# Keys turned on TensorE instead of VectorE, weight words split without GpSimd, and more of them split during the first attention

## The chip, the cores and the metric

The kernel runs on one core of one Trainium2 chip. The metric is the device time of one execution in microseconds. An execution uses five engines with an instruction queue each, all served in order: TensorE (PE, with its weight loads PEld), VectorE (DVE), ScalarE (ACT), GpSimd (POOL) and SyncE (SP), which here only issues DMAs. ScalarE issues some DMAs too. Sixteen DMA engines carry out the transfers of all queues.

## The reference

```python
def sm_attn(qq, kk, vv):
    s = scale * np.matmul(qq, kk.transpose(0, 1, 3, 2))
    s = s - np.max(s, axis=-1, keepdims=True)
    a = np.exp(s)
    a = a / (np.sum(a, axis=-1, keepdims=True) + 1e-09)
    return np.matmul(a, vv)

p_packed = sm_attn(p, k, v)             # 32 packed queries read 576 keys; batch 8, heads 8, width 64
out = sm_attn(q, p_packed, p_packed)    # 576 queries read the 32 packed values
x = out.transpose(0, 2, 1, 3).reshape(4608, 512)
h = x @ w_in;  x = (h * np.cos(h)) @ w_out          # first layer, 512 -> 2048 -> 512
h = x @ w_in2                                       # second layer, the same sizes
P = a[0] + a[1] * h + a[2] * h**2 + a[3] * h**3
Q = 1.0 + abs(b[0]) * abs(h) + abs(b[1]) * h**2
return (P / (Q + 1e-6)) @ w_out2
```

The four weight matrices are given in 64-bit floating point; everything else is fp32.

## The kernel before

**Precision.** The large products use TensorE's fp32r type. An operand is kept as two tiles, a rounded `hi` and a rest `lo`, and each product is three matmuls (hi·hi, hi·lo, lo·hi; `PASSES`). `split` (line 65) makes the pair from fp32 data: a copy on ScalarE and a difference on VectorE. `convert` (line 74) makes it from 64-bit weights, 128x512 of them at a time. It sees each weight as two 32-bit words, `up` and `dn`, interleaved in memory. ScalarE turns `dn` into a scaled float (line 80); VectorE makes an fp32 number of `up` by shifts and masks (lines 82 and 87) and takes its exponent out (line 90); GpSimd multiplies the scaled `dn` by that power of two (line 91); VectorE adds it (line 92); ScalarE rounds the sum to `hi` (line 93); GpSimd takes the difference `lo` (line 94). There are 64 such conversions: 16 of the first layer's input weights (`conv_w1i`), 16 of its output weights (`conv_w1o`) and 32 of the second layer's (`conv_w2`). The words come by a 512 KB load each (`load_st`, tag `st64`, three buffers); for the first layer ScalarE's queue issues it.

**Stage one, the attention (lines 125 to 450).** The 64 heads go in 16 groups of four. For a group `n`, `load_k` and `load_v` fetch its keys and values (SP's queue; two buffers for k, three for v). `prep` turns k with two VectorE transposes of 32x32 blocks (line 185). The packed queries `p` are loaded once (line 149), and VectorE sets them into a block-diagonal tile `pbd` (lines 169 to 176). `s1` makes the scores of four heads in four fp32 matmuls of 288 columns with all 128 rows (line 194), takes the maximum on VectorE (line 208) and the exponential on ScalarE (line 213). The score tile is two PSUM banks with two buffers. `et` turns the exponentials on TensorE by six transposes (line 229); `pv` multiplies them with v in four column tiles (line 242); `ppt` turns the packed values and splits them into `wl` (lines 264 to 279). PSUM's eight banks are all taken: four by `s1`, two by `et`, one each by `pv` and `pt`. Inside the same loop run the conversions: `cvs` lists them in order, `conv_next` does the next and starts the load three places on. There are `NA` = `OF` + `RING` = 7 + 3 = 10 that belong to this stage, at two of three steps of the loop. The second attention of batch 0 (`attn2_steps`, line 307) runs in its last steps and borrows the score tile's PSUM.

**Stage two, the folding (lines 645 to 660).** `wunit(x)` multiplies the packed values of all batches with one 128x512 piece of the first layer's input weights, 12 matmuls and four copies, and stores the four results to DRAM (`wd`); `load_wq` reads them back, and they take the place of attention times weights. 16 units, with the remaining conversions between them: a piece for `RING` units ahead, an output-weight conversion at nine of the units (`more`), and the first four slots of the next stage.

**Stage three, the first layer (128 slots, line 613).** Each slot has 12 matmuls of `h` (line 537), a chain over ScalarE and VectorE for h·cos h (lines 556 to 572), and 24 matmuls of `y` (line 584) of two slots before. The second attention of the next batch and, at every third slot, one of the 32 conversions of the second layer's weights run beside it. **Stage four, the second layer (144 slots, lines 680 to 778)** has neither attention nor conversions.

The order on each engine is set ahead of the run by a planner that simulates the instructions (line 804). It keeps dependencies and may move an instruction past others of the program; `hold` (line 54) ties some to an earlier matmul in that order.

Of the kernel before, what the change touches and what calls it, by code (L numbers as in the profile page):

```python
# [20 lines left out]
def pack_attention_moe_moe_kernel(  # L21
# [14 lines left out]
    nc = tc.nc  # L36
    B, H, S, D = q.shape
    M = p.shape[2]
# [35 lines left out]
    def convert(hi, lo, wd64, pool, n, until=None):  # L74
        up, dn = wd64[:, :, 1], wd64[:, :, 0]
        f = pool.tile([128, n], U32, tag="cvf", bufs=2, name="cvf")
        pw = pool.tile([128, n], U32, tag="cvp", bufs=2, name="cvp")
        dl = dn.bitcast(F32)
        ff, pf = f.bitcast(F32), pw.bitcast(F32)
        hold(nc.scalar.activation(out=dl, in_=dn, func=AF.Copy, scale=2.0 ** -52), until)  # L80
        hold(
            nc.vector.tensor_scalar(  # L82
                out=f, in0=up, scalar1=3, scalar2=0x3FFFFFFF, op0=ALU.logical_shift_left, op1=ALU.bitwise_and
            ),
            until,
        )
        nc.vector.scalar_tensor_tensor(  # L87
            out=f, in0=up, scalar=0xC0000000, in1=f, op0=ALU.bitwise_and, op1=ALU.bitwise_or
        )
        nc.vector.tensor_scalar(out=pw, in0=f, scalar1=0xFF800000, scalar2=None, op0=ALU.bitwise_and)  # L90
        nc.gpsimd.tensor_tensor(out=pf, in0=dl, in1=pf, op=ALU.mult)  # L91
        nc.vector.tensor_tensor(out=ff, in0=ff, in1=pf, op=ALU.add)
        nc.scalar.activation(out=hi, in_=ff, func=AF.Copy)
        nc.gpsimd.tensor_tensor(out=lo, in0=ff, in1=hi.bitcast(F32), op=ALU.subtract)
# [18 lines left out]
    if True:  # L113
# [35 lines left out]
        nc.sync.dma_start(out=px, in_=p.rearrange("b (g h) m d -> (h m) (b g) d", g=G))  # L149
        nc.sync.dma_start(out=par[:, 0:4], in_=pa.unsqueeze(0).to_broadcast([128, 4]))  # L150
        nc.sync.dma_start(out=par[:, 4:6], in_=pb.unsqueeze(0).to_broadcast([128, 2]))
        nc.vector.tensor_scalar(out=coef[:, 0:4], in0=par[:, 0:4], scalar1=-1.0, scalar2=None, op0=ALU.mult)
# [9 lines left out]
        make_identity(nc, ident)  # L162
# [5 lines left out]

        pbd = wv.tile([128, NG, NDB, 4, M], F32, name="pbd")
        nc.gpsimd.memset(pbd, 0.0)  # L170
        for n0, n1 in ((0, 2), (2, NG)):
            for h in range(4):
                nc.vector.transpose(
                    out=pbd[32 * h:32 * h + 32, n0:n1, :, h],
                    in_=px[32 * h:32 * h + 32, n0:n1].rearrange("p n (e i) -> p n e i", e=NDB),
                )

        kT_t = {}

        def prep(n):  # L180
            b, g = divmod(n, G)
            kT = wk.tile([128, NDB, 6, 3, 32], F32, tag="kT", bufs=2, name="kT")
            kx = kx_t.pop(n)
            for e in range(NDB):
                nc.vector.transpose(  # L185
                    out=kT[:, e].rearrange("p r a j -> p a r j"),
                    in_=kx[:, :, 32 * e:32 * e + 32].rearrange("p (a r) i -> p a r i", a=3),
                )
            kT_t[n] = kT.rearrange("p e r a j -> p e (r a j)")
# [11 lines left out]

        E_t, rd_t = {}, {}

        def s1(n):
            ps = ps0.tile([128, 2, 512], F32, tag="s1", bufs=2, name="s1")
            scores(ps, pbd[:, n].rearrange("p e h m -> p e (h m)"), kT_t.pop(n))
# [12 lines left out]
            nc.vector.reciprocal(out=rd, in_=sm)  # L219
            E_t[n], rd_t[n] = E, rd  # L220
# [15 lines left out]
        def pv(n):  # L236
# [3 lines left out]
            for r in range(6):  # L240
                for h in range(4):
# [3 lines left out]
                        rhs=vx[:, h, r * D:r * D + D],  # L245
# [132 lines left out]
        RING = 3  # L378
# [21 lines left out]
        OF = 7  # L400
        cvs = [(load_w1o, conv_w1o, f) for f in range(OF)] + [(load_w1i, conv_w1i, x) for x in range(RING)]
        NA = len(cvs)
        more = (0, 2, 4, 7, 9, 10, 13, 14, 15)
# [16 lines left out]
        for i in range(3):  # L420
# [4 lines left out]
            0, wk, lambda nm: ps0.tile([128, 2, 512], F32, tag="s1", bufs=2, name=nm), tg0, lambda: None  # L425
# [3 lines left out]
        for n in range(NG + 1):  # L429
# [13 lines left out]
            if n % 3 and at_cv[0] < NA:  # L443
                conv_next()
# [156 lines left out]
        a_p.append(wk)  # L601
# [58 lines left out]
        e0.close()  # L660
        at_p = e1t.enter_context(tc.tile_pool(name="at", bufs=1, side="right", **RW))
# [147 lines left out]
```

## Time and profile before

| | |
|---|---|
| median of 3 runs | 1685.23 us (1684.16 to 1691.55) |
| profiled execution | 1685.26 us, span 1683.5 us |
| TensorE busy | 1587.0 us (94% of the span) |
| VectorE busy | 1327.3 us (79%) |
| ScalarE busy | 1197.9 us (71%) |
| GpSimd busy | 184.7 us (11%) |
| granted TensorE clock, mean | 0.979 |

Busy times are those of one profiled execution. Matmuls are pipelined, so the records overlap, and the time of a block of matmuls says more than a record's length. A fp32 matmul shows as two records. In a row of grouped instructions the columns are: line, engine, operation, written tile <- read tiles, shapes, how many; busy time and mean length in ns of one; then the idle time of the engine just before them and what ended it.

### The profile page before, as it was taken

Reading aid. Unit: us, or ns where it says so; the run is one execution under the profiler, and the core shown is the slowest. Engines: PE = TensorE matmul, PEld = TensorE weight load, DVE = VectorE, ACT = ScalarE, POOL = GpSimd, SP = SyncE. Lnnn points to the kernel's source line nnn. Section 1 sums busy time; section 2 is a strip of 40 time slices with the busy share of each in tenths; the row PEclk is TensorE's granted clock in tenths of the full one; section 3 lists DMA queues with packets and bytes.
Section 4 is the critical chain, followed back from the end, with each engine's and each line's share of the span. In section 5 each row is a group of like instructions: output and inputs, shape, how many; then the busy total and the mean of one; then the engine's idle time right before and its main releaser. Section 6 shows DMA issues by size and latency. Waiting matters only on the chain.

```text
span 1683.5 us, 25095 instructions
## 1 busy us (share of the span) xinstructions
PE 1587.0 (94%) x9408; PEld 1382.6 (82%) x9408; DVE 1327.3 (79%) x2054; ACT 1197.9 (71%) x1933; POOL 184.7 (11%) x140
## 2 busy tenths in 40 slices
PE   5677879999999999999999999999999999999996
PEld 3555769999999999999998888888888888888884
DVE  7866977787878787878558888888888888888884
ACT  3345656686767676868668777777787878787874
POOL 4304530121111111221000000000000000000000
PEclk9888899999999999999999999999999999999998
DMA  9977744453435444435183101010100102020100
GB/s 280 260 205 263 254 167 122 129 152 127 141 126 154 140 139 146 137 125 188 62 297 134 52 25 50 26 50 26 51 26 26 50 1 76 1 75 1 45 6 25
DMA packets 104377, 183.57 MB, mean 109 GB/s; under 512 B 12096, under 2 KB 46912, under 8 KB 104256
## 3 DMA queue, kind: packets, MB, share of 16 engines
q1 hardware_dynamic: 97344, 163.09, 30.4%
q10 hardware_dynamic: 6912, 18.88, 3.6%
q8 instruction: 74, 1.21, 0.3%
q14 instruction: 47, 0.39, 0.1%
HBM read 117.97 MB, written 63.96 MB: 108 GB/s over the span
## 4 chain that ended last, share of the span: by engine, by line
PE 81%; DVE 8%; DMA 4%; ACT 3%; issue 2%; POOL 1%; ACTq 0%; SPq 0%; POOLq 0%; DVEq 0%
PE h L689 24%; PE o L747 23%; PE y L584 21%; PE h L537 10%; PE s L194 2%; DMA st<-in_moe_w_in_dram 1%; DVE cvf L87 1%; PE w L290 1%; DVE cvf L82 1%; DMA qx<-in_q_dram 1%; DMA wd<-wev 1%; DVE g L569 1%; DMA px<-in_p_dram 1%; DVE kT L185 1%; ACT u L562 0%
## 5 line engine op out<-in xcount | busy, mean ns | idle before, releaser
L584 PE MATMUL y<-gh,w1o 128*128 128x288 f32 x2048 | 433.3, 298 | 0.8 <-ACT gh L66 0.4
L689 PE MATMUL h<-x,w 128*128 128x512 f32 x1728 | 422.2, 393 | 0.0
L689 PEld LDWEIGHTS h<-x,w 128*128 128x128 f32 x1728 | 324.2, 188 | 74.2
L584 PEld LDWEIGHTS y<-gh,w1o 128*128 128x128 f32 x2048 | 337.2, 189 | 3.4 <-DVE yl L67 1.1
L747 PE MATMUL o<-w,g2h 128*128 128x512 f32 x1152 | 332.9, 393 | 1.2 <-ACT g2h L707 1.2
L584 PE MATMUL y<-gl,w1o 128*128 128x288 f32 x1024 | 297.1, 296 | 2.4 <-DVE gl L67 2.4
L747 PEld LDWEIGHTS o<-w,g2h 128*128 128x128 f32 x1152 | 216.1, 188 | 51.1 <-ACT g2h L707 2.1
L537 PE MATMUL h<-ah,wq 128*128 128x288 f32 x1024 | 227.8, 299 | 15.4 <-DVE g L569 7.1
L747 PE MATMUL o<-w,g2l 128*128 128x512 f32 x576 | 199.9, 393 | 0.0
L722 ACT ACTIVATE sq<-h 128x512 f32<-128x512 f32 x144 | 87.2, 606 | 156.4 <-PE h L689 156.4
L584 PEld LDWEIGHTS y<-gl,w1o 128*128 128x128 f32 x1024 | 193.9, 189 | 3.9 <-DVE gl L67 3.3
L537 PEld LDWEIGHTS h<-ah,wq 128*128 128x128 f32 x1024 | 172.6, 190 | 21.0 <-issue 10.6
L724 DVE SCALAR_TENSOR_TENSOR ab<-sq,coef,ab 128x512 f32<-128x512 f32 x144 | 108.2, 751 | 66.8 <-ACT ab L723 66.6
L562 ACT ACTIVATE u<-h,coef 128x576 f32<-128x576 f32 x128 | 94.2, 737 | 87.7 <-PE h L537 86.9
L537 PE MATMUL h<-al,wq 128*128 128x288 f32 x512 | 151.8, 297 | 0.0
L569 DVE SCALAR_TENSOR_TENSOR g<-h,r 128x576 f32<-128x576 f32 x128 | 96.2, 754 | 61.2 <-ACT r L568 61.0
L91 POOL TENSOR_TENSOR cvp<-st,cvp 128x512 f32<-128x512 f32 x64 | 90.1, 1408 | 442.4 <-DVE cvp L90 191.8
L733 DVE SCALAR_TENSOR_TENSOR ab<-ab,y 128x512 f32<-128x512 f32 x144 | 99.6, 691 | 48.5 <-ACT y L730 48.5
L747 PEld LDWEIGHTS o<-w,g2l 128*128 128x128 f32 x576 | 108.1, 188 | 24.7
L563 DVE SCALAR_TENSOR_TENSOR r<-u,h 128x576 f32<-128x576 f32 x128 | 95.5, 748 | 37.3 <-ACT u L562 36.6
L725 ACT ACTIVATE c<-h,coef 128x512 f32<-128x512 f32 x144 | 113.9, 791 | 8.4 <-DVE g2l L713 8.4
L67 DVE TENSOR_TENSOR gl<-g,gh 128x576 fp32r<-128x576 f32 x128 | 102.8, 803 | 21.4 <-ACT gh L66 19.7
(88 smaller groups left out, 2453.1 us busy)
## 6 DMA issues: line engine op xcount, KB each, us to landing
x<-yd SPq DMA_DIRECT2D x36, 512.0 KB
w<-w2d SPq DMA_DIRECT2D x68, 256.0 KB
wd<-wev SPq DMA_DIRECT2D x64, 256.0 KB
wq<-wd SPq DMA_DIRECT2D x64, 256.0 KB
kx<-in_k_dram SPq DMA_DIRECT2D x16, 576.0 KB
vx<-in_v_dram SPq DMA_DIRECT2D x48, 192.0 KB
qx<-in_q_dram SPq DMA_DIRECT2D x16, 576.0 KB
yd<-yh SPq DMA_DIRECT2D x64, 144.0 KB
```

The costliest lines, as they stand in the source:

```text
L67: lo_eng.tensor_tensor(out=lo, in0=src, in1=hi.bitcast(F32), op=ALU.subtract)
L91: nc.gpsimd.tensor_tensor(out=pf, in0=dl, in1=pf, op=ALU.mult)
L537: last_h[0] = nc.tensor.matmul(out=ps[:, u, 0:HS], lhsT=wq[:, g, a, o:o + 128], rhs=a_t[b, g][c][:, hf * HS:hf * HS + HS], start=(i == 0), ...
L562: nc.scalar.activation(out=u, in_=ph, func=AF.Identity, bias=coef[:, 6:7])
L563: nc.vector.scalar_tensor_tensor(out=r, in0=u, scalar=RND, in1=ph, op0=ALU.subtract, op1=ALU.subtract)
L569: nc.vector.scalar_tensor_tensor(out=gt, in0=ph, scalar=2.0 * math.pi, in1=r, op0=ALU.mult, op1=ALU.mult)
L584: nc.tensor.matmul(out=y_t[d][:, 0:HS], lhsT=w1o_s[f // 4][a][:, f % 4, 128 * d:128 * d + 128], rhs=gs[c][:, u], start=(f == 0 and i == 0) ...
L689: nc.tensor.matmul(out=ps, lhsT=w2_s[f][:, 0, a, 128 * kk:128 * kk + 128], rhs=x_t[t, c, kk], start=(i == 0), stop=(i == 3 * NKD - 1),)
L724: nc.vector.scalar_tensor_tensor(out=ab, in0=sq, scalar=coef[:, 5:6], in1=ab, op0=ALU.mult, op1=ALU.add)
L725: nc.scalar.activation(out=c1, in_=ph, func=AF.Identity, scale=coef[:, 3:4], bias=coef[:, 2:3])
L733: nc.vector.scalar_tensor_tensor(out=ab, in0=ab, scalar=QC, in1=y0, op0=ALU.add, op1=ALU.mult)
L747: nc.tensor.matmul(out=o_t[s], lhsT=g2_t[n][a][:, 128 * s:128 * s + 128], rhs=w2_s[f][:, 1, c], start=(f == 0 and i == 0), stop=(f == NFC ...
```

## The change

1. `convert`: without GpSimd and with one ScalarE instruction in place of two. VectorE's first two instructions make an fp32 number with the low twelve bits of its word cut off (`0x3FFFF000`), so that it is `hi` already; ScalarE copies it. The cut bits (`up & 0x1FF`, in place) and `dn` are put together as integers and scaled by the exponent to `lo`. VectorE has six instructions in place of four.
2. k and p are turned by ten TensorE transposes per group into PSUM (tag `tp`, two buffers of one bank), and ScalarE copies them out in four instructions. The scores are eight matmuls of 64 rows and 32 columns of weights, each in its own tile of the array. The score tile has one buffer in place of two. v's row blocks are read in the order that this makes.
3. p is loaded in two pieces, and doubled along the free axis by VectorE (two groups) and GpSimd (the rest); `pbd` is gone. The identity matrix is made before the first coefficients.
4. `OF` 7 to 12, `RING` 3 to 5: 17 conversions in the attention stage, one at every step of its loop; four output-weight conversions left for the folding stage, at units 11 to 14.
5. The second pair of buffers of the turned attention is allocated after the folding stage instead of before it.

```diff
@@ convert
-        hold(nc.scalar.activation(out=dl, in_=dn, func=AF.Copy, scale=2.0 ** -52), until)
...
-                out=f, in0=up, scalar1=3, scalar2=0x3FFFFFFF, op0=ALU.logical_shift_left, op1=ALU.bitwise_and
+                out=f, in0=up, scalar1=3, scalar2=0x3FFFF000, op0=ALU.logical_shift_left, op1=ALU.bitwise_and
...
+        nc.scalar.activation(out=hi, in_=ff, func=AF.Copy)
+        nc.vector.tensor_scalar(out=up, in0=up, scalar1=0x1FF, scalar2=None, op0=ALU.bitwise_and)
         nc.vector.tensor_scalar(out=pw, in0=f, scalar1=0xFF800000, scalar2=None, op0=ALU.bitwise_and)
-        nc.gpsimd.tensor_tensor(out=pf, in0=dl, in1=pf, op=ALU.mult)
-        nc.vector.tensor_tensor(out=ff, in0=ff, in1=pf, op=ALU.add)
-        nc.scalar.activation(out=hi, in_=ff, func=AF.Copy)
-        nc.gpsimd.tensor_tensor(out=lo, in0=ff, in1=hi.bitcast(F32), op=ALU.subtract)
+        nc.vector.scalar_tensor_tensor(out=q, in0=up, scalar=2.0 ** 32, in1=dn, op0=ALU.mult, op1=ALU.add)
+        nc.vector.scalar_tensor_tensor(out=lo, in0=q, scalar=2.0 ** -52, in1=pf, op0=ALU.mult, op1=ALU.mult)
@@ p
-        nc.sync.dma_start(out=px, in_=p.rearrange("b (g h) m d -> (h m) (b g) d", g=G))
+        pv4 = p.rearrange("b (g h) m d -> (h m) (b g) d", g=G)
+        nc.sync.dma_start(out=px[:, 0:2], in_=pv4[:, 0:2])
+        nc.sync.dma_start(out=px[:, 2:NG], in_=pv4[:, 2:NG])
+        pxx = wv.tile([128, NG, 2, D], F32, name="pxx")
+        for n0, n1, eng in ((0, 2, nc.vector), (2, NG, nc.gpsimd)):
+            eng.tensor_copy(out=pxx[:, n0:n1], in_=px[:, n0:n1].unsqueeze(2).to_broadcast([128, n1 - n0, 2, D]))
@@ prep
-            for e in range(NDB):
-                nc.vector.transpose(
...
+            blocks = [kx[:, a, s].rearrange("p t d -> p (t d)") for s in range(3) for a in range(3)]
+            blocks.append(pxx[:, n].rearrange("p t d -> p (t d)"))
+            for i0 in (0, 4, 8):
+                ps = ps0.tile([128, 4, 128], F32, tag="tp", bufs=2, name="tp")
+                m = min(4, 10 - i0)
+                for i in range(m):
+                    nc.tensor.transpose(ps[:, i], blocks[i0 + i], ident)
+                w = min(4, 9 - i0)
+                nc.scalar.activation(out=kT[:, i0:i0 + w], in_=ps[:, 0:w], func=AF.Copy)
+                if w < m:
+                    nc.scalar.activation(out=pT, in_=ps[:, w], func=AF.Copy)
@@ scores of s1
+        def scores1(ps, kT, pT):
+            for t in range(2):
+                for h in range(4):
+                    nc.tensor.matmul(
+                        out=ps[32 * h:32 * h + 32, t, 0:HS],
+                        lhsT=pT[64 * t:64 * t + 64, 32 * h:32 * h + 32],
+                        rhs=kT[64 * t:64 * t + 64, :, 32 * h:32 * h + 32],
+                        start=True,
+                        stop=True,
+                        tile_position=(64 * t, 32 * h),
+                    )
-            ps = ps0.tile([128, 2, 512], F32, tag="s1", bufs=2, name="s1")
+            ps = ps0.tile([128, 2, 512], F32, tag="s1", bufs=1, name="s1")
@@ plan
-        RING = 3
+        RING = 5
-        OF = 7
+        OF = 12
-        more = (0, 2, 4, 7, 9, 10, 13, 14, 15)
+        more = (11, 12, 13, 14)
-            if n % 3 and at_cv[0] < NA:
+            if at_cv[0] < NA:
```

## Rows read from the trace of the kernel before

**Rows 1.** Busy time, clock and DMA share of the four stages.
```profile
core 0: us, PE busy (x) PEld busy (x) DVE busy (x) ACT busy (x) POOL busy (x), PEclk, DMA share, GB/s
0.00:127.80 127.80, 81.90 (x1041) 59.69 (x1041) 96.85 (x213) 48.34 (x95) 37.77 (x36) 0.89 0.87 246
127.80:240.00 112.20, 87.40 (x368) 64.53 (x369) 88.46 (x114) 69.79 (x114) 56.51 (x40) 0.87 0.77 255
240.00:866.00 626.00, 616.39 (x4520) 606.51 (x4519) 479.44 (x716) 448.51 (x675) 90.39 (x64) 1.00 0.44 139
866.00:1683.50 817.50, 801.29 (x3484) 651.86 (x3482) 662.51 (x1012) 631.29 (x1049) 0.00 (x0) 0.99 0.13 44
```

**Rows 2.** The same view of the folding stage's last 20 us.
```profile
220.00:240.00 20.00, 11.85 (x47) 8.15 (x48) 14.12 (x20) 12.74 (x21) 7.94 (x6) 0.86 0.65 211
```

**Rows 3.** Groups of VectorE's instructions, 320 to 800 us: the conversions.
```profile
L87 DVE SCALAR_TENSOR_TENSOR cvf<-st,cvf 128x512 uint32<-128x512 uint32 x30 | 20.5, 684 | 0.4
L92 DVE TENSOR_TENSOR cvf<-cvf,cvp 128x512 f32<-128x512 f32 x30 | 20.3, 676 | 1.9 <-POOL cvp L91 1.9
L90 DVE TENSOR_SCALAR cvp<-cvf 128x512 uint32<-128x512 uint32 x30 | 12.6, 419 | 0.1
L82 DVE TENSOR_SCALAR cvf<-st 128x512 uint32<-128x512 uint32 x30 | 12.5, 417 | 0.0
```

**Rows 4.** The same groups, 127.8 to 240 us.
```profile
L87 DVE SCALAR_TENSOR_TENSOR cvf<-st,cvf 128x512 uint32<-128x512 uint32 x19 | 21.6, 1135 | 0.3
L92 DVE TENSOR_TENSOR cvf<-cvf,cvp 128x512 f32<-128x512 f32 x19 | 20.0, 1059 | 2.9 <-POOL cvp L91 2.9
L82 DVE TENSOR_SCALAR cvf<-st 128x512 uint32<-128x512 uint32 x19 | 12.9, 681 | 4.8 <-POOL w1i L94 4.8
L90 DVE TENSOR_SCALAR cvp<-cvf 128x512 uint32<-128x512 uint32 x19 | 11.4, 599 | 0.3
```

**Rows 5.** Groups of VectorE's instructions, 0 to 127.8 us: turns and conversions.
```profile
L185 DVE STREAM_TRANSPOSE kT<-kx 128x576 f32<-128x576 f32 x32 | 22.8, 750 | 5.7 <-DMA kx<-in_k_dram 5.7
...
L87 DVE SCALAR_TENSOR_TENSOR cvf<-st,cvf 128x512 uint32<-128x512 uint32 x13 | 11.9, 913 | 0.1
L92 DVE TENSOR_TENSOR cvf<-cvf,cvp 128x512 f32<-128x512 f32 x13 | 10.2, 788 | 0.6 <-POOL cvp L91 0.5
...
L90 DVE TENSOR_SCALAR cvp<-cvf 128x512 uint32<-128x512 uint32 x13 | 6.7, 513 | 0.0
L82 DVE TENSOR_SCALAR cvf<-st 128x512 uint32<-128x512 uint32 x13 | 6.4, 495 | 4.0 <-POOL w1o L94 4.0
L173 DVE STREAM_TRANSPOSE pbd<-px 32x128 f32<-32x128 f32 (+1 forms) x8 | 5.6, 702 | 2.9 <-DMA px<-in_p_dram 2.7
```

**Rows 6.** Groups of ScalarE's instructions, 0 to 127.8 us.
```profile
L80 ACT ACTIVATE st<-st 128x512 f32<-128x512 uint32 x16 | 10.7, 672 | 33.2 <-DMA st<-in_moe_w_in_dram 15.8 <-DMA vx<-in_v_dram 7.5 <-DMA st<-in_moe_w_out_dram 4.2
...
L66 ACT ACTIVATE wl<-pt 128x128 fp32r<-128x128 f32 x16 | 4.4, 272 | 10.7 <-PE pt L275 10.3 <-DVE cvf L92 0.3
```

**Rows 7.** ScalarE's copies out of PSUM, 127.8 to 240 us.
```profile
L301 ACT ACTIVATE wev<-w 128x512 f32<-128x512 f32 x48 | 27.8, 591 | 16.1 <-PE w L290 12.3 <-POOL cvp L91 1.7 <-DMA wd<-wev 1.4
```

**Rows 8.** Timeline, 111 to 119 us: start, duration, engine, line.
```profile
111.61 2.11 PE L194 MATMUL s<-kT,pbd 128*128 128x288 f32 x8
...
113.75 0.76 DVE L208 TENSOR_REDUCE mx<-s 128x1 f32<-128x576 f32 x1
113.86 0.71 PEld L242 LDWEIGHTS pv<-vx,eT 96*32 96x32 f32 x48 [0.17 <-PE s L194]
113.86 0.88 PE L242 MATMUL pv<-vx,eT 96*32 96x64 f32 x48
...
114.67 0.86 PE L229 MATMUL et<-ident,E 128*96 128x128 f32 x6
...
118.03 0.74 ACT L213 ACTIVATE E<-s,nb 128x576 f32<-128x576 f32 x1 [0.48 <-DVE nb L210]
```

**Rows 9.** Groups of TensorE's instructions, 0 to 127.8 us: the first scores.
```profile
L194 PE MATMUL s<-kT,pbd 128*128 128x288 f32 x128 | 43.8, 495 | 23.7 <-DVE pbd L173 13.3 <-DVE kT L185 10.4
```

**Rows 10.** Who waited for whom on TensorE, 240 to 866 us: total, times, longest.
```profile
PE h L537 <- DVE g L569: 7.1, 10, 1.2
```

More of the change, by code (lines that the diff above doesn't have):

```diff
@@ L77, in convert @@
         pw = pool.tile([128, n], U32, tag="cvp", bufs=2, name="cvp")
-        dl = dn.bitcast(F32)
-        ff, pf = f.bitcast(F32), pw.bitcast(F32)
-        hold(nc.scalar.activation(out=dl, in_=dn, func=AF.Copy, scale=2.0 ** -52), until)
+        ff, pf, q = f.bitcast(F32), pw.bitcast(F32), dn.bitcast(F32)
         hold(
             nc.vector.tensor_scalar(
-                out=f, in0=up, scalar1=3, scalar2=0x3FFFFFFF, op0=ALU.logical_shift_left, op1=ALU.bitwise_and
+                out=f, in0=up, scalar1=3, scalar2=0x3FFFF000, op0=ALU.logical_shift_left, op1=ALU.bitwise_and
             ),
@@ L148, in pack_attention_moe_moe_kernel @@
         px = wv.tile([128, NG, D], F32, tag="vx", bufs=3, name="px")
-        nc.sync.dma_start(out=px, in_=p.rearrange("b (g h) m d -> (h m) (b g) d", g=G))
+        pv4 = p.rearrange("b (g h) m d -> (h m) (b g) d", g=G)
[4 more added lines that the diff above has]
+            eng.tensor_copy(out=pxx[:, n0:n1], in_=px[:, n0:n1].unsqueeze(2).to_broadcast([128, n1 - n0, 2, D]))
         nc.sync.dma_start(out=par[:, 0:4], in_=pa.unsqueeze(0).to_broadcast([128, 4]))
         nc.sync.dma_start(out=par[:, 4:6], in_=pb.unsqueeze(0).to_broadcast([128, 2]))
+        make_identity(nc, ident)
         nc.vector.tensor_scalar(out=coef[:, 0:4], in0=par[:, 0:4], scalar1=-1.0, scalar2=None, op0=ALU.mult)
@@ L161, in pack_attention_moe_moe_kernel @@
         load_v(0)
-        make_identity(nc, ident)
         nc.gpsimd.memset(mask, 0.0)
@@ L167, in pack_attention_moe_moe_kernel @@
         load_k(2)
[L169 to L172, printed above, removed]
-                nc.vector.transpose(
-                    out=pbd[32 * h:32 * h + 32, n0:n1, :, h],
-                    in_=px[32 * h:32 * h + 32, n0:n1].rearrange("p n (e i) -> p n e i", e=NDB),
-                )
         kT_t = {}
         def prep(n):
-            b, g = divmod(n, G)
-            kT = wk.tile([128, NDB, 6, 3, 32], F32, tag="kT", bufs=2, name="kT")
-            kx = kx_t.pop(n)
-            for e in range(NDB):
[L185 to L189, printed above, removed]
+            kx = kx_t.pop(n).rearrange("p (a s t) d -> p a s t d", a=3, t=2)
+            kT = wk.tile([128, 9, 128], F32, tag="kT", bufs=2, name="kT")
+            pT = wk.tile([128, 128], F32, tag="pT", bufs=2, name="pT")
+            blocks = [kx[:, a, s].rearrange("p t d -> p (t d)") for s in range(3) for a in range(3)]
[9 more added lines that the diff above has]
+                    nc.scalar.activation(out=pT, in_=ps[:, w], func=AF.Copy)
+            kT_t[n] = (kT, pT)
         def scores(ps, lhs, rhs):
@@ L200, in scores @@
                     )
+        def scores1(ps, kT, pT):
[9 more added lines that the diff above has]
+                    )
         E_t, rd_t = {}, {}
         def s1(n):
-            ps = ps0.tile([128, 2, 512], F32, tag="s1", bufs=2, name="s1")
-            scores(ps, pbd[:, n].rearrange("p e h m -> p e (h m)"), kT_t.pop(n))
+            ps = ps0.tile([128, 2, 512], F32, tag="s1", bufs=1, name="s1")
+            scores1(ps, *kT_t.pop(n))
             mx = wk.tile([128, 1], F32, tag="mx", bufs=2, name="mx")
@@ L244, in pv @@
                         lhsT=eT[:, r, 32 * h:32 * h + 32],
-                        rhs=vx[:, h, r * D:r * D + D],
+                        rhs=vx[:, h, (2 * (r % 3) + r // 3) * D:(2 * (r % 3) + r // 3 + 1) * D],
                         start=(r == 0),
@@ L424, in pack_attention_moe_moe_kernel @@
         at = attn2_steps(
-            0, wk, lambda nm: ps0.tile([128, 2, 512], F32, tag="s1", bufs=2, name=nm), tg0, lambda: None
+            0, wk, lambda nm: ps0.tile([128, 2, 512], F32, tag="s1", bufs=1, name=nm), tg0, lambda: None
         )
@@ L600, in pack_attention_moe_moe_kernel @@
         wk = e1k.enter_context(tc.tile_pool(name="work1", bufs=1, **RW))
-        a_p.append(wk)
         ehp, e1t = ExitStack(), ExitStack()
@@ L660, in pack_attention_moe_moe_kernel @@
         e0.close()
+        a_p.append(e1k.enter_context(tc.tile_pool(name="a1", bufs=1, **RW)))
         at_p = e1t.enter_context(tc.tile_pool(name="at", bufs=1, side="right", **RW))
```

## The prediction, made before the changed kernel was run

> **What bounds the kernel now.** I read the table of stages first [rows 1]. From 240 us on TensorE is busy for 616.4 of 626.0 and then for 801.3 of 817.5 us at a granted clock of 0.99 to 1.00: nothing can be won there except the few idle microseconds. The two stages ahead of it are different. In the attention (0 to 127.8 us) TensorE is busy for 81.9 us, VectorE for 96.9, ScalarE for 48.3; the 16 DMA engines are the fullest, 0.87 of the stretch. In the folding stage (127.8 to 240 us: the products of the packed values with the first weights, written to DRAM as `wd`) TensorE has 87.4 of 112.2 us, VectorE 88.5, ScalarE 69.8, GpSimd 56.5, DMA 0.77. So no engine is at its limit in either; in-order queues pass waits to each other while DMA is the nearest floor. The last 20 us of the folding stage are the emptiest (TensorE 11.85 us, DMA 0.65) [rows 2]: the last `wd` must reach DRAM and come back. What follows starts when this stage ends, so a microsecond off it is a microsecond off the end.
>
> **A conversion, old and new.** It is the piece that moves between all the stages. Where GpSimd is seldom in the way its four VectorE instructions cost 0.684 + 0.676 + 0.419 + 0.417 = 2.20 us [rows 3]; in the folding stage, with GpSimd busy half of the time, the same four cost 1.135 + 1.059 + 0.681 + 0.599 = 3.47 us [rows 4], and in the attention 0.913 + 0.788 + 0.513 + 0.495 = 2.71 [rows 5]. The change takes both GpSimd instructions out, so I charge the undisturbed prices: shift-and 0.417, or 0.684, the new in-place mask 0.417 (same shape and stride as the shift), exponent mask 0.419, and the two new scalar-tensor-tensors 0.684 each: 3.3 us. Both ends: the in-place mask could run as slowly as a two-operand instruction (0.684) and the conversion from strided integers could cost 0.913 (the dearest undivided row near it), 3.8 us; not below 2.9, four old prices and two of the cheap kind. ScalarE loses one of its two instructions, 0.672 us [rows 6].
>
> **The attention stage.** VectorE: out go the 32 turns of k (22.8 us), the eight of p (5.6) and 13 old conversions (13 x 2.71 = 35.2); in come 17 x 3.3 = 56.1. 96.9 - 63.6 + 56.1 = 89.4 us [rows 1, 5]. ScalarE: out 10.7 (16 first instructions) [rows 6]; in, for each of 16 groups, two copies of a 128x512 bank at 0.591 [rows 7] and two of 128x128 at 0.272 [rows 6], 27.6 us in all, and four more of the remaining conversion copies, 2.4 at the same price: 68 us. TensorE: six transposes take 0.86 us, so ten take 1.43 and 160 take 22.9 [rows 8]. The new score products are not in the trace. Eight records of the old ones take 2.11 us, 0.264 each, so sixteen one after the other take 4.2; side by side in eight tiles they could take 0.5. The nearest row is the value product, already in four column tiles: 48 records of 64 columns would need 48 x 0.264 x 64/288 = 2.8 us in turn and take 0.88, a factor of 3.2 [rows 8]. I take 4.2/3.2 = 1.3. Per group 1.43 + 1.3 against 2.11: 10 us more over 16 groups, 92 of some 130 us. No engine becomes the bound by its sum.
>
> Changing between whole-array and tiled products shows as 0.17 us in front of the value product, whose weights wait for the last score; the transposes behind it begin at 114.67 while its block runs to 114.74, so leaving costs nothing visible [rows 8]. I charge 0.17 for entering. The Trainium skill (TensorEngine Tiling (Array Packing), Key Properties) says that every change of tiling mode drains the engine, entering and leaving; by that a round costs another 0.17, and 19 rounds (below) another 3 us: 1677 in place of 1674. The trace agrees for entering only.
>
> DMA: 0.87 x 127.8 = 111 us of work. In this stage 16 words had already been read (16 first instructions on ScalarE [rows 6]), though the program's own order asks for 10 conversions and three loads ahead; after, it asks for 17 and three. Four more words then, at most seven; one is 0.524 MB, and 246/0.87 = 283 GB/s make it 1.85 us: 7.4 us (13.0 at most), 119 us of transfers. Idle were 16.6 us; I leave 14 of them, for the run-out at the end needs no transfer: 133 us.
>
> The second way to the same figure is the score buffer, of which there is now one. A round is scores, maximum, exponential, and only then the next scores; the second block's two score products use the same buffer. One round of before goes from 111.61 to 118.77 us (118.03 + 0.74), 7.2 us, of which the scores are 2.11 and the two instructions 1.5; the rest is waiting in queues [rows 8]. With the new scores it is 7.2 - 2.11 + 1.3 + 0.17 = 6.5. The start: the first scores wait 13.3 us, until p is turned, 5.6 us of instructions [rows 5, 9]; the small first load of p and the transposes on TensorE end that, and I take 4 us off (bounds 0 and 8.5, the turning and the 2.9 us of waiting for p). 18 rounds and one more for what follows the last: 9.3 + 19 x 6.5 = 133 us. Both ways: **+5 us**. Bounds: -9 (all idle filled, 119) and +13 (seven words, idle as it was), and the rival below.
>
> Waits added. The first instruction of a conversion is now VectorE's, so the wait for its word stands there; until now ScalarE took it, 27.5 us in all (15.8 + 7.5 + 4.2) [rows 6]. Behind it on VectorE stand the maximum and the reciprocals; 89.4 us of work leave 43 for it. On GpSimd the copy of p waits for its second load with the identity written behind it; if the planner kept that order the transposes would begin with it, at worst the 4 us that I take off at the start. On TensorE the transposes of a late k block the value product behind them, as VectorE's turns did the maximum (5.7 us [rows 5]). SP issues one load more.
>
> **The folding stage.** 19 conversions stand in it, 66.0 us of VectorE [rows 4]; after, 15 are asked for, 49.5: 88.5 - 16.5 = 72. ScalarE: 69.8 - 16 x 0.672 - 4 x 0.591 = 57. GpSimd: 56.5 to nothing. DMA: 0.77 x 112.2 = 86.4 us, less four words at 0.524 MB / (255/0.77 = 331 GB/s) = 1.6 us each, 80. That is now the highest sum. Of the 25.8 us in which DMA idles, 7 lie in the last 20 us and stay [rows 2]; waits for GpSimd before VectorE (7.7 us [rows 4]) and for outputs (on ScalarE 12.3 us for products, which wait for it in turn [rows 7]) shrink. I keep 15: 95 us, **-17 us**. Bounds: -6 (idle as it was, 106) and -22 (90).
>
> **The first layer.** 32 conversions go from 2.20 to 3.3 us on VectorE: +35 us on 479.4, spread over some 480 of the 626 us, while ScalarE loses 21.5. That stage has 9.6 us without TensorE, 7.1 of them ten waits for VectorE's `g` [rows 1, 10]. VectorE goes from 0.77 to 0.82 of the stage: cover remains, and I take **+1 us** (0 to +35 if every added microsecond reached TensorE). The second layer has none of this: 0.
>
> **Sum.** The profiled execution took 1685.3 us (span 1683.5); the median of the runs is 1685.2, so nothing is corrected. 1685 + 5 - 17 + 1 = **1674 us**.
>
> **Rivals.**
> - *More is won*: the queues were what left DMA idle, and without GpSimd it fills. Attention -6, folding -18: 1661. For it speaks that VectorE's four instructions stretch by half beside GpSimd; against it that the attention's transfers grow.
> - *The words only change places*: seven more in the attention (+13), and the folding stage, held by its own stores and the way back of the last `wd`, gives 13: 1686. For it speaks the DMA share, near its top in both.
> - *The single score buffer sets the attention.* A round of 7.7 us makes 9.3 + 19 x 7.7 = 156, +28: 1685 + 28 - 17 + 1 = 1697. The price per 0.1 us of round is 1.9 us; from 7.5 us on the kernel is slower than before by over 0.5%. For it speaks the round of 7.2 us with VectorE no more loaded than it will be, and the word waits that move onto VectorE; against it that in that round nobody was waiting for it, since a second buffer lay ready.
> - *VectorE holds back the first layer*: half of its 35 us reach TensorE through `g`: 1674 + 18 = 1692.
>
> **Chances.** Forecast 0.50 (its own range 1662 to 1683), more won 0.17, places only 0.13, score buffer 0.12, first layer 0.08. About 0.5%, 8.4 us, is what a measurement of this kernel can tell from no change; the lines are 1676.8 and 1693.6. Faster: 0.36 of the forecast's 0.50, 0.17, and 0.02 of places only: 0.55. Slower: the score buffer's 0.12, 0.05 of the first layer's and 0.02 of others: 0.19. Within: 0.26. The range leaves out the better half of "more won" and most of the score buffer: 1659 to 1696.
>
> **What would show it.** The first products of the folding stage start near 133 us and its end lies near 228. A conversion's six VectorE instructions sum to 3.3 us at a nearly constant length of each. Scores take about 1.3 us and a round under 7. If the first stage ends after 150 us with one score waiting for the exponential before it, the buffer was the price; if waits for `g` grow beyond 15 us, the first layer was. A folding stage of over 105 us says that conversions were not what held it.

## The result and the profile after

The changed kernel is slower by 0.6%: 1698.8 us median (1693.4 to 1699.9) against 1684.7 us (1684.2 to 1691.6) on the same chip, ratio 1.0062 with a 95% interval of 1.0043 to 1.0082. I had forecast 1674 us. Its profiled execution has a span of 1697.0 us, 13.5 more than before.

The stages of the changed kernel, busy time of each engine with granted clock, DMA share and GB/s, cut where the kernel before was cut; they answer to [rows 1]:

```profile
core 0: us, PE busy (x) PEld busy (x) DVE busy (x) ACT busy (x) POOL busy (x), PEclk, DMA share, GB/s
0.00:138.60 138.60, 92.06 (x1328) 62.02 (x1328) 94.90 (x234) 64.52 (x149) 3.66 (x12) 0.82 0.85 242
138.60:244.70 106.10, 81.75 (x368) 60.55 (x369) 67.86 (x118) 56.61 (x92) 0.00 (x0) 0.93 0.76 250
244.70:879.80 635.10, 620.71 (x4522) 610.89 (x4522) 499.85 (x780) 432.55 (x643) 0.00 (x0) 0.99 0.44 138
879.80:1697.00 817.20, 801.01 (x3482) 652.25 (x3480) 662.38 (x1012) 631.31 (x1049) 0.00 (x0) 0.99 0.13 44
```

Read the first column of each row against its neighbour of before: the attention is 10.8 us longer (127.8), the folding 6.0 us shorter (112.1 when it is cut at the same instruction), the first layer 8.7 us longer (626.4), the second layer the same to 0.1 us. Read then the last two columns: in the attention the DMA share is 0.85 where it was 0.87, in the folding 0.76 where it was 0.77. The engines' loads changed by up to 56 us, and the transfers went at the rate they had.

Where a table below needs the stages of many kernels, they are cut by three starts that every trace has: the first product of the folding units, their last, and the first product of the second layer. For before that gives 127.8 / 101.1 / 637.4 us, for the changed kernel 138.6 / 93.4 / 647.8. The last third holds the way back of the last stores as well.

In the attention, who waited for whom (total, times, longest):

```profile
DVE cvf L81 <- DMA st<-in_moe_w_out_dram: 19.0, 9, 5.5
...
PE tp L186 <- DMA kx<-in_k_dram: 13.5, 6, 6.3
...
PE s L207 <- ACT E L227: 3.4, 3, 1.5
```

VectorE's first instruction of a conversion waits 19.0 us for its word, with another 3.7 for the input weights' words; the scores wait only 3.4 us for the exponential that frees the one score buffer. So the word waits did move onto VectorE, and the buffer did not become the bound.

The folding stage's part of the chain that ended last (start, length, what):

```profile
143.89 6.08 DMA wd<-wev
...
151.32 5.39 DMA wd<-wev
...
159.93 6.10 DMA wd<-wev
...
174.37 3.68 DMA wd<-wev
...
202.76 3.77 DMA wd<-wev
...
206.76 6.96 DMA wd<-wev
...
230.08 3.37 DMA wd<-wev
```

Seven times, 35 us together, the chain goes through the store of a unit's result. The reason stands in the waits of that stage:

```profile
PEld w L304 <- ACT wev L315: 21.1, 25, 2.8
...
ACT wev L315 <- DMA wd<-wev: 16.8, 10, 2.7
```

ScalarE's copy of a product waits 16.8 us for a store to free one of the four `wev` buffers, and TensorE waits for that copy. Before, the same wait was 1.4 us [rows 7]; VectorE, which copies the other products out, had 3.2 us of it before and has 1.8 now.

In the first layer TensorE's waits for `g` [rows 10] have doubled:

```profile
PE h L551 <- DVE g L583: 14.0, 11, 3.7
```

and its longest wait (3.68 us, ending at 530.05) shows what such a wait does beside the idle time itself:

```profile
520.00:530.00 10.00, 6.37 (x48) 6.14 (x47) 8.51 (x15) 8.40 (x11) 0.00 (x0) 1.00 0.72 202
530.00:540.00 10.00, 9.95 (x63) 9.98 (x64) 9.86 (x16) 7.96 (x12) 0.00 (x0) 0.83 0.29 81
```

TensorE is busy for 6.37 of 10 us, and in the next 10 us its granted clock is 0.83. The same follows the second longest wait, from 780 to 790 us. Cut at full tens, no other 10 us between 250 and 860 us are below 1.00, and in the kernel before none are. TensorE's busy time over the stage rose by 3.9 us (616.8 to 620.7) for the same 4522 records; idle rose by 4.8 us (9.6 to 14.4).

What VectorE did ahead of the `g` that TensorE waited for:

```profile
523.63 1.35 DVE L363 TENSOR_REDUCE sm<-sT 128x36 f32<-128x1152 f32 x1 [1.24 <-ACT sT L361]
524.90 1.41 DVE L577 SCALAR_TENSOR_TENSOR r<-u,h 128x576 f32<-128x576 f32 x2
...
526.85 1.43 DVE L368 TENSOR_TENSOR sT<-sT,sm 128x576 f32<-128x576 f32 x2
528.20 0.77 DVE L372 STREAM_TRANSPOSE aT<-sT 128x576 f32<-128x576 f32 x1
529.15 1.43 DVE L583 SCALAR_TENSOR_TENSOR g<-h,r 128x576 f32<-128x576 f32 x2 [0.18 <-ACT r L582]
```

No conversion stands there. Between the chain's own `r` and `g` it is the second attention (`sm`, `sT`, `aT`), in an order that the planner gave. The same instructions stand ahead of the second longest wait, 2.64 us; conversion instructions stand ahead of three shorter ones (1.0, 1.6 and 1.6 us).

### The profile page after: what moved, and what is told of

It is laid out like the page before. It is cut to its first block, busy times and chain, and to the rows that moved or that the text cites. A ratio compares the mean times of both kernels' runs of the same rounds, so it can differ in the third digit from the quotient of the medians.

```text
span 1697.0 us, 25527 instructions
## 1 busy us (share of the span) xinstructions
PE 1595.5 (94%) x9696; PEld 1385.7 (82%) x9696; DVE 1325.0 (78%) x2143; ACT 1185.0 (70%) x1933; POOL 3.7 (0%) x12
## 4 chain that ended last, share of the span: by engine, by line
PE 80%; DVE 7%; DMA 7%; ACT 4%; issue 1%; SPq 0%; ACTq 0%; DVEq 0%
PE h L703 24%; PE o L761 23%; PE y L598 19%; PE h L551 10%; DMA st<-in_moe_w_out_dram 2%; DMA wd<-wev 2%; PE w L304 1%; PE s L196 1%; ACT r L582 1%; DVE g L583 1%; DVE r L577 1%; ACT r L581 1%; DMA wq<-wd 1%; DVE cvf L86 1%; DMA kx<-in_k_dram 0%
## 5 line engine op out<-in xcount | busy, mean ns | idle before, releaser
L551 PE MATMUL h<-ah,wq 128*128 128x288 f32 x1024 | 231.5, 302 | 24.3 <-DVE g L583 14.0
L576 ACT ACTIVATE u<-h,coef 128x576 f32<-128x576 f32 x128 | 94.2, 738 | 88.2 <-PE h L551 87.8
L581 ACT ACTIVATE r<-r 128x576 f32<-128x576 f32 x128 | 87.3, 683 | 50.4 <-DVE r L577 50.2
L739 ACT ACTIVATE c<-h,coef 128x512 f32<-128x512 f32 x144 | 114.0, 791 | 8.3 <-DVE g2l L727 8.3
L740 ACT ACTIVATE c<-h,coef 128x512 f32<-128x512 f32 x144 | 114.7, 796 | 0.0
```

The lines of the kernel that those rows point to most:

```text
L551: last_h[0] = nc.tensor.matmul(out=ps[:, u, 0:HS], lhsT=wq[:, g, a, o:o + 128], rhs=a_t[b, g][c][:, hf * HS:hf * HS + HS], start=(i == 0), ...
L576: nc.scalar.activation(out=u, in_=ph, func=AF.Identity, bias=coef[:, 6:7])
L581: nc.scalar.activation(out=r, in_=r, func=AF.Abs)
L739: nc.scalar.activation(out=c1, in_=ph, func=AF.Identity, scale=coef[:, 3:4], bias=coef[:, 2:3])
L740: nc.scalar.activation(out=c0, in_=ph, func=AF.Identity, scale=coef[:, 1:2], bias=coef[:, 0:1])
```

## The experiments

There are sixteen runs. Each is compared with runs of the kernel before on the same chip, whose median was 1688.1 to 1689.8 us there. Stages are given as first unit product / units / from the last unit product to the second layer, in us of one profiled execution.

| kernel | stages | span | ratio to before (95%) |
|---|---|---|---|
| before | 127.8 / 101.1 / 637.4 | 1683.5 | 1 |
| changed | 138.6 / 93.4 / 647.8 | 1697.0 | 1.0062 (1.0043 to 1.0082) |
| c_convert_only | 124.6 / 98.4 / 647.2 | 1687.4 | 1.0037 (1.0024 to 1.0050) |
| k_turn_only | 123.2 / 103.8 / 637.2 | 1681.4 | 1.0006 (0.9987 to 1.0024) |
| s_plan_only | 141.7 / 95.8 / 641.2 | 1695.8 | 1.0057 (1.0036 to 1.0077) |
| ks_turn_and_plan | 139.1 / 91.7 / 640.9 | 1688.9 | 1.0000 (0.9987 to 1.0014) |
| ck_convert_and_turn | 123.3 / 99.0 / 645.7 | 1685.0 | 1.0008 (0.9994 to 1.0022) |
| ck_old_in_layer | 124.3 / 98.4 / 638.7 | 1678.6 | 0.9971 (0.9959 to 0.9983) |
| all_old_in_layer | 137.9 / 94.2 / 639.6 | 1688.9 | 1.0020 (1.0011 to 1.0029) |
| before_longer_in_layer | 128.2 / 103.1 / 649.7 | 1698.1 | 1.0057 (1.0042 to 1.0072) |
| all_half_words | 130.2 / 96.5 / 645.7 | 1689.5 | 1.0020 (1.0002 to 1.0037) |
| all_hi_only | 130.5 / 93.1 / 645.8 | 1686.5 | 0.9998 (0.9982 to 1.0013) |
| ck_old_more_outputs | 132.7 / 88.5 / 639.6 | 1678.0 | 0.9907 (0.9874 to 0.9941) |
| ck_old_fewer_words | 116.0 / 109.4 / 637.6 | 1680.2 | 0.9970 (0.9955 to 0.9985) |
| all_four_ahead | 138.3 / 99.4 / 645.8 | 1700.7 | 1.0051 (1.0036 to 1.0066) |
| all_four_ahead_stores | 135.6 / 83.3 / 645.5 | 1681.6 | 0.9970 (0.9957 to 0.9984) |
| ck_old_more_outputs2 | 127.3 / 85.9 / 637.4 | 1667.8 | 0.9876 (0.9861 to 0.9891) |
| ck_old_fewer_words_stores | 116.3 / 99.6 / 639.1 | 1672.2 | 0.9912 (0.9898 to 0.9926) |

### Each part alone, and two of them together

The first four kernels are the kernel before with the `convert` hunk alone (c), with the hunks of p, `prep`, `scores1` and the score buffer alone (k), with the plan alone (s: the lines below and the later pool), and the changed kernel with the old `convert` (ks). The expectations name three theories: A, the conversion is the cost; B, the turn on TensorE with its single score buffer; C, the words moved into the attention.

```diff
-        RING = 3
+        RING = 5
-        OF = 7
+        OF = 12
-        more = (0, 2, 4, 7, 9, 10, 13, 14, 15)
+        more = (11, 12, 13, 14)
-            if n % 3 and at_cv[0] < NA:
+            if at_cv[0] < NA:
```

> The kernel before with the new conversion alone (VectorE's six instructions, no GpSimd); keys still turned on VectorE, plan and score buffers as before. Stages of before: attention to 127.8 us, folding 112 us, first layer 626 us; of the changed kernel: 138.6, 106, 635. Theory A (the conversion is the cost: the wait for its word now stands on VectorE, and 35 us of VectorE work go into the first layer): attention ends at 133 us or later with some 10 us of VectorE waiting for words, folding 104, first layer 635, 1690 us. Rival B (the score buffer and the TensorE transposes are the cost in the attention): attention stays within 2 us of 128, folding 104, first layer 635, 1686 us. Rival C (the words moved into the attention are its cost): as B, since no word is moved here.

> The kernel before with the keys and the packed queries turned on TensorE and one score buffer alone; conversion and plan as before. Theory A: attention 128 us or a little less, since VectorE loses 28 us of turning; first layer 626; 1683 us. Rival B: attention 136 us or more with TensorE waiting for exponentials and copies, folding 112, 1694 us. Rival C: as A.

> The kernel before with the plan alone: 17 conversions of the old kind in the attention, 15 left for the folding, second attention buffers allocated later. Theory A and rival B: attention 131 us, folding 108, first layer 626, 1684 us. Rival C (words in the transfer-bound stage are the cost): attention 136 us or more, folding no shorter than 108, 1690 us.

> The changed kernel with the old conversion (GpSimd in it, the word's first reader on ScalarE again). Theory A: attention 131 us, folding 107, first layer 626, 1682 us. Rival B: attention 138 us as in the changed kernel, folding 107, first layer 626, 1689 us. Rival C: attention 136 to 138 us too, 1689 us; the two are told apart by the kernels with one of the two parts alone.

Two profiles of one and the same kernel differ by 5 us in the attention (see the folding stage below), so one difference of that size says little. With the changed kernel and ck_convert_and_turn (below), however, each part can be read in three pairs, with it and without it:

| part | attention with / without, us |
|---|---|
| conversion | 124.6 / 127.8, 123.3 / 123.2, 138.6 / 139.1 |
| turn, single score buffer | 123.2 / 127.8, 123.3 / 124.6, 139.1 / 141.7 |
| plan | 141.7 / 127.8, 139.1 / 123.2, 138.6 / 123.3 |

Theory A fell for the attention: the conversion lengthens it in no pair by more than 0.1 us (VectorE waits 2.9 us for words in c_convert_only, where some 10 were expected). It held for the first layer (+9.8 us). Rival B fell: the turn with its single buffer lengthens nothing. Rival C held: the plan lengthens the attention by 13.9, 15.9 and 15.3 us, and gives back 5.3, 12.1 and 5.6 in the folding.

The traces also give the loads of words issued by the first unit product: 16 before and in k_turn_only, 14 in c_convert_only and ck_convert_and_turn, 20 in the changed kernel, 22 in s_plan_only and ks_turn_and_plan. So the plan adds six loads to this stage, not the seven that later expectations count, and two loads fewer may be all that made c_convert_only's attention shorter than that of before.

### The first layer

Two kernels keep the old form for the 32 conversions of the second layer's weights (a second function, `convert_old`, with the text of before); one adds work to the kernel before.

```diff
@@ ck_old_in_layer, all_old_in_layer
-            convert(hi, lo, st_t.pop(("w2", i)), cv_p, 512, last_h[0])
+            convert_old(hi, lo, st_t.pop(("w2", i)), cv_p, 512, last_h[0])
@@ before_longer_in_layer: in the conversions of that stage alone, lines 87 to 90 a second time
+        nc.vector.scalar_tensor_tensor(
+            out=f, in0=up, scalar=0xC0000000, in1=f, op0=ALU.bitwise_and, op1=ALU.bitwise_or
+        )
+        nc.vector.tensor_scalar(out=pw, in0=f, scalar1=0xFF800000, scalar2=None, op0=ALU.bitwise_and)
```

> New conversion and keys on TensorE, plan of before. So far the stages read (first unit product / units / from the last unit product to the second layer): before 127.8 / 101.1 / 637.4, conversion alone 124.6 / 98.4 / 647.2, turn alone 123.2 / 103.8 / 637.2, plan alone 141.7 / 95.8 / 641.2, turn and plan 139.1 / 91.7 / 640.9, all three 138.6 / 93.4 / 647.8. If the parts add up (conversion -3.2, -2.7, +9.8; turn -4.6, +2.7, -0.2): 120 / 101 / 647, span 1685, no change against before. If the plan is what the waits for words need (theory A's remainder): attention 128 or more, 1693.

> As the kernel with new conversion and turn, but the 32 conversions of the second layer's weights keep the old form. If the first layer's loss belongs to the new conversion standing in it: 120 / 101 / 637, span 1675, faster than before by 0.5%. If it comes from what the earlier stages leave behind: first layer 645 as with the new form, span 1684.

> The changed kernel with the old form of the second layer's 32 conversions. Conversion as the first layer's cost: 138.6 / 93.4 / 641 (the 641 of the two kernels with the plan and the old conversion), span 1690. Otherwise 648 stays and the span is 1697.

> The kernel before with two of VectorE's instructions done twice in each of the 32 conversions of the second layer's weights (the same values again): 1.1 us more on VectorE for each, as the new form has, with GpSimd and both ScalarE instructions kept. If VectorE's added load is the cost: first layer 645 to 648, waits of TensorE for g about 14 us, span 1692. If the new form's shape is (one engine in place of three, another order): 638, waits for g 7 to 8 us, span 1684.

Conversion and turn do not add up in the attention (123.3, as either alone). The layer is clear: with the old form it is 638.7 and 639.6, with the new one 645.7 to 647.8, and 1.1 us more of VectorE per conversion, with GpSimd and ScalarE as they were, makes it 649.7. So it is the new conversion inside this stage that costs, and work added to VectorE is enough for a loss of that size. The waits for `g`, first of ck_old_in_layer, then of before_longer_in_layer:

```profile
PE h L573 <- DVE g L605: 7.1, 10, 1.2
```

```profile
PE h L563 <- DVE g L595: 11.7, 16, 2.1
```

7.1 us as before; 11.7 us with the added instructions, between the two forecasts (14, and 7 to 8).

The control adds more than the new form does. In the last third VectorE is busy for 485.6 us before, 505.1 in the changed kernel and 525.5 in before_longer_in_layer: +19.4 against +39.9. The new form should have added 35, but with GpSimd idle other instructions of VectorE are shorter (`gl` takes 0.822 us before and 0.752 after, 320 to 800 us). And the new form's longest wait is 3.7 us, the control's 2.1. So whether the load as such, the new form's shape or the order that the planner makes of either sets the loss is not shown; the two longest waits speak for the order.

### The attention

In all_half_words six of the word loads are left out and their conversions read the word before; in all_hi_only every word is loaded, and for the same six weights only `hi` is made.

```diff
@@ all_half_words
+            if f < OF and f % 2 == 1:
+                st_t[f] = last_st[0]
+                return
@@ all_hi_only: after hi, for odd f below OF, in place of the rest
+        nc.gpsimd.memset(lo.bitcast(F32), 0.0)
@@ ck_old_fewer_words, against ck_old_in_layer
-        OF = 7
+        OF = 4
-        more = (0, 2, 4, 7, 9, 10, 13, 14, 15)
+        more = (0, 1, 2, 4, 5, 7, 8, 10, 11, 13, 14, 15)
```

> The changed kernel with six word loads of 512 KB left out: the odd output weights of the first twelve are converted from the words of the one before (so those weights are not the given ones), every conversion still runs. Attention ended at 138.6 us. If the words' transfers are the cost (seven loads more took 13.9 us with the old conversion alone and 15.9 beside the turn, 2.0 to 2.3 us a load): six loads less end it near 126. If the conversions' work or their place in the queues is the cost: within 3 us of 138.

> The changed kernel with all word loads, but for the same six weights only the rounded part is made and the rest is set to zero by GpSimd: four VectorE instructions less for each, 13 us of VectorE in the attention. If transfers are the cost: attention stays within 3 us of 138.6. If VectorE's work is the cost: it ends near 126 to 130.

> The same kernel (124.3 / 98.4 / 638.7) with three conversions less in the attention and three more in the folding stage (seven and twelve output weights after it). If a word costs 2.0 to 2.3 us in the attention and gives back 1.7 in the folding, as the two kernels with the plan said: attention 118, folding 103.5, span 1677, no difference that can be told. If the attention is no longer held by transfers: 124 / 103, span 1683.

Neither pure theory holds. Six loads less gave 8.4 us, not 12.6; all loads with four VectorE instructions less in six conversions gave 8.1. The medians of all executions agree that both help: 1.0020 and 0.9998 against the changed kernel's 1.0062. The rows of the attention in these two kernels:

```profile
0.00:130.20 130.20, 83.58 (x1329) 58.05 (x1329) 94.58 (x234) 63.51 (x149) 3.69 (x12) 0.87 0.82 234
```

```profile
0.00:130.50 130.50, 86.84 (x1329) 61.12 (x1329) 87.23 (x210) 65.58 (x149) 6.00 (x18) 0.84 0.92 258
```

With fewer loads the same VectorE work leaves DMA emptier (0.82, 234 GB/s); with less VectorE work DMA fills (0.92, 258 GB/s). So both count: a word costs its transfer and its place in VectorE's queue, where the maxima stand behind it. ScalarE's exponentials wait 9.9 us for the maximum's result (`nb`) in the changed kernel, 9.8 with fewer loads and 4.9 with less VectorE work. How the price divides between the two is not shown. Ten conversions and eleven loads in place of 13 and 14 end the attention at 116.0 us (124.3).

### The folding stage

The buffers of the units' results, in three kernels; all_four_ahead is the control that makes room for them in the changed kernel.

```diff
@@ ck_old_more_outputs, ck_old_more_outputs2, ck_old_fewer_words_stores
-                t = we_p.tile([128, 512], F32, tag="wev", bufs=4, name="wev")
+                t = we_p.tile([128, 512], F32, tag="wev", bufs=8, name="wev")
@@ all_four_ahead
-        RING = 5
+        RING = 4
@@ all_four_ahead_stores: that, and
-                t = we_p.tile([128, 512], F32, tag="wev", bufs=4, name="wev")
+                t = we_p.tile([128, 512], F32, tag="wev", bufs=7, name="wev")
```

> The kernel with new conversion and turn, plan of before and old form in the layer (124.3 / 98.4 / 638.7, span 1678.6), with eight buffers instead of four for the results of the folding units. If the wait for stores to free these buffers holds the folding stage, as the chain of the changed kernel has it (seven such waits, 35 us): folding 90 to 93, span 1672. If DMA or the products hold it and the wait only stands last: 97 to 99, span 1678.

> Control: the changed kernel with four input-weight pieces ahead instead of five (16 conversions asked for in the attention). By the rate of some 245 GB/s at which both stages went in every kernel, one word of 0.524 MB less: attention 136, folding 95, first layer 647, span 1696.

> The same with seven buffers instead of four for the folding units' results. If their stores hold the folding stage: folding 85 to 88 (it fell by 9.9 us with eight in the other kernel) at a transfer rate above 265 GB/s, span 1688. If conversions, products or DMA hold it: 93 to 96.

> The same kernel once more. If the attention's 132.7 us belonged to that execution: near 124, folding 88.5, span 1670. If it belongs to the order that the planner gave this kernel: 131 to 134 again, span 1678.

> Three conversions less in the attention (116.0 / 109.4 with four buffers) and eight buffers. If the gains add up: attention 116, folding 99, first layer 638, span 1671. If the folding is then held by its twelve plus thirteen conversions: 107, span 1678.

The units' stretch without and with the added buffers, otherwise the same kernel:

```profile
138.30:237.70 99.40, 81.12 (x347) 60.41 (x348) 65.57 (x117) 50.56 (x83) 0.00 (x0) 0.87 0.76 249
```

```profile
135.60:218.90 83.30, 74.91 (x348) 56.70 (x348) 64.60 (x117) 50.35 (x83) 0.00 (x0) 0.96 0.89 304
```

The same instructions on every engine, and 16.1 us less (14.2 us between the medians of all executions, 1699.2 and 1685.0); the transfer rate goes from 249 to 304 GB/s. TensorE's busy time is 6.2 us less at a granted clock of 0.96 in place of 0.87. In ScalarE's rows of waits the wait for a store falls from 12.9 to 1.9 us:

```profile
ACT wev L315 <- DMA wd<-wev: 12.9, 9, 3.6
```

```profile
ACT wev L315 <- DMA wd<-wev: 1.9, 1, 1.9
```

So four buffers held the folding stage of the changed kernel. The control missed its expectation: its units took 99.4 us, not 95. The 245 GB/s that it took for both stages fit the attention alone; with four buffers the units went at 247 to 279. With eight buffers, the turn, the new conversion and the old one in the first layer, the kernel beats both: 1668.5 us, ratio 0.9876. Without the added buffers that kernel is at 0.9971 (ck_old_in_layer). The kernel before was not run with eight buffers, so how much of the gain it would have had by that line alone is open. Two executions of that same program show 132.7 and 127.3 us of attention and 88.5 and 85.9 of units, so a difference of 5 us in the attention between two profiles is no finding by itself. Twelve weights in the folding stage cost more than they save in the attention (99.6 against 85.9 us of units, 116.3 against 127.3; ratios 0.9912 and 0.9876, with intervals that do not meet).

## Why the prediction was wrong

Three terms were too low: the folding by 11.0 us, the attention by 5.8, the first layer by 7.7. That is 24.5 of the 24.8 us between 1674 and 1698.8.

**The conversion's price was right.** Its six VectorE instructions measure, in the first layer, 0.418 + 0.682 + 0.421 + 0.418 + 0.683 + 0.679 = 3.3 us, the forecast sum. The in-place mask and the two new scalar-tensor-tensors had no row before; the mask and the first of the two, grouped over 320 to 800 us:

```profile
L92 DVE SCALAR_TENSOR_TENSOR st<-st 128x512 f32<-128x512 uint32 x31 | 21.2, 683 | 0.0
...
L90 DVE TENSOR_SCALAR st<-st 128x512 uint32<-128x512 uint32 x31 | 13.1, 421 | 0.2
```

**Folding, -17 forecast, -6.0 measured: the largest error.** VectorE fell to 67.9 us (72 forecast, for 15 conversions; 13 are left there), ScalarE to 56.6 (57), GpSimd to nothing. The step that failed is "Of the 25.8 us in which DMA idles ... I keep 15". DMA idles 25.5 us after the change. I took the waits for GpSimd and for products as what had kept it idle; when they shrank, the next in line was the ring of four store buffers, which the profile of before showed with 1.4 us on ScalarE's row [rows 7] and in its folding chain with three stores. I named stores only in a rival. With seven or eight buffers the units take 83.3 to 88.5 us (101.1 before), and most or all of the drop that I forecast is there. The sign that I had named came true: a folding stage of over 105 us says that conversions were not what held it, and it took 106.1.

**Attention, +5 forecast, +10.8 measured.** Four more words were loaded by its end, as forecast (20 loads issued against 16), and the sum of the transfers was right too (0.85 of 138.6 us is 118 us; 119 forecast). "Idle were 16.6 us; I leave 14 of them" failed: 20.8 us are idle. The kernels with 13 conversions in this stage end it at 123 to 133 us, those with 18 or 19 and all of their loads and work at 136 to 142, and all of them move 230 to 258 GB/s. An estimate from this: at the changed kernel's 242 GB/s four words of 0.524 MB take 8.7 of the 10.8 us; they came at the rate of the stage, not into its gaps. The moves of work were near the forecast (VectorE 94.9 us where I had 89.4, for 19 conversions where I counted 17; ScalarE 64.5 where I had 68). The score round was not the price: 16 records take 0.71 us where I took 1.3, and k_turn_only has the single buffer and is early. So my second way to +5, 19 rounds of 6.5 us, met the first by chance: with the same single buffer the stage ends at 123.2 us there and at 116.0 in ck_old_fewer_words.

Entering and leaving tiled products, once more. In the timeline the transposes behind the scores start at 123.01 us, while the scores' block runs to 122.37 + 0.71 = 123.08: no idle time of TensorE shows on leaving. But the ends of such blocks are modelled, and the weight load of these transposes has stood idle for 0.47 us. The same stands behind the three score blocks before (loads at 108.47, 112.00 and 116.56); each load starts 0.07 to 0.08 us before the block's end. Behind a block of whole-array transposes the next load runs ahead (121.51, where that block ends at 121.12 + 0.66 = 121.78). The Trainium skill (TensorEngine Tiling (Array Packing), Key Properties) has a drain at every change of tiling mode; the trace agrees as far as the load is not run ahead, and shows no price for it, so the 3 us of the prediction's sentence are neither borne out nor excluded.

```profile
122.37 0.71 PE L207 MATMUL s<-kT,pT 64*32 64x288 f32 x16
...
123.01 0.42 PEld L186 LDWEIGHTS tp<-ident,kx 128*128 128x128 f32 x4 [0.47 <-issue]
123.01 0.66 PE L186 MATMUL tp<-ident,kx 128*128 128x128 f32 x4
```

The ten transposes are dearer than forecast, 32.2 + 5.5 = 37.7 us of busy time for 160 (144 of k and 16 of p) where I took 22.9. I had the price of six in a row at full clock (0.86 us); they come in three pieces, of which four transposes take 0.66 us, and the granted clock of the stage is 0.82, where it was 0.89. TensorE has room for it: it is busy for 92.1 of 138.6 us. That my sum of 92 us was met is chance: dearer transposes beside cheaper scores (15.2 us for 16 rounds where I had 20.8). The two groups of TensorE's instructions in this stage:

```profile
L186 PE MATMUL tp<-ident,kx 128*128 128x128 f32 x144 | 32.2, 362 | 20.9 <-DMA kx<-in_k_dram 13.5 <-ACT kT L188 7.3
...
L207 PE MATMUL s<-kT,pT 64*32 64x288 f32 x256 | 15.2, 543 | 4.8 <-ACT E L227 3.4 <-ACT pT L190 1.4
```

**First layer, +1 forecast, +8.7 measured.** "VectorE goes from 0.77 to 0.82 of the stage: cover remains" is the step that failed. VectorE is only 0.79 busy there (+20 us, not +35), yet `g` stands in its queue behind whatever came first, and TensorE's wait for it went from 7.1 to 14.0 us; the longest single wait from 1.2 to 3.7. That covers the 4.8 us of added idle time. The other 3.9 us are added busy time, with the clock at 0.83 after the two longest waits. I had the mechanism as the last rival at 0.08 and half of 35 us; 8.7 us arrived, a quarter.

**The rivals.** In number the single score buffer came nearest, 1697, and that is luck: its attention of 156 us and its waits for exponentials did not come (138.6 us, and 3.4 us of waits). In mechanism the nearest was the words that only change places, 1686: it had the attention (+13) nearly right, it named the folding stage's own stores, and it had the folding (-13) too good.

## What to carry to other kernels

The shares of 0.77 to 0.87 on the DMA engines were what the queues and buffers of these stages let through, not room. Before counting a gain from work taken off an engine, look for the ring of buffers that waits for a store or load, even one with a small wait now, and price the stage at its own rate, not at the rate of its busy time (here 242 GB/s in the attention, not the 283 that I took). An engine's average share says little about a dependent instruction that sits in its in-order queue: here the waits behind it doubled as the share went from 0.77 to 0.79. Look at what stands ahead of it in the queue. Undo a bundle part by part: here the parts measured +0.4%, 0 and +0.6%, and more store buffers, which none of them contained, were worth 0.8% in the changed kernel (1.0051 to 0.9970).

## What the runs showed of the hardware that was not expected

- TensorE's granted clock was 0.83 in the 10 us behind each of the two longest waits of the first layer (3.68 and 2.64 us), and 1.00 in all other 10 us between 250 and 860 us; in the kernel before, with waits of at most 1.2 us, it was 1.00 throughout. The added busy time of the stage is nearly as much as the added idle time (3.9 beside 4.8 us).
- The weight load of whole-array transposes stood idle for 0.47 us behind tiled score products, at all four places that the timeline has between 107.8 and 125 us; behind whole-array transposes it ran 0.27 us ahead.
- GpSimd's absence gave VectorE its undisturbed prices back in the folding stage: the shift-or instruction takes 0.69 us there, 1.135 before [rows 4]. In the first layer `gl` takes 0.752 us, 0.822 before.
